# Expert weights split only in a branch where the expert changes, and 1.15 instead of 3.2 channel units beside each expert block

## The chip, the cores and the metric

The kernel runs on one core of a Trainium2 chip. The metric is the device time of one execution in microseconds. The profiled execution is one execution with its own time; the median of three others is given beside it.

## What is computed

Three stages follow each other on 4608 tokens of width 512. An attention with pooled keys gives the rows `x`. A mixture of eight experts then gives each token one expert: a fresh arg-max of its logits, or that of the token before it where the local gate says so. Last comes a layer norm with a channel feed-forward network on every token, with a residual.

```python
for b in range(B):
    prev_e = -1
    for s in range(S):
        fresh_e = int(np.argmax(logits[b, s]))
        if s == 0 or local_gate[b, s] < 0.5:
            e = fresh_e
        else:
            e = prev_e if prev_e >= 0 else fresh_e
        prev_e = e
        h = np.maximum(x[b, s] @ w1[e], 0.0)
        out[b, s] = p[e] * (h @ w2[e])
...
ch = np.maximum(xn @ w_ch1, 0.0) @ w_ch2
return (x + ch).astype(np.float32)
```

`w1[e]` is 512 x 1024 and `w2[e]` 1024 x 512, `w_ch1` 512 x 2048 and `w_ch2` 2048 x 512. For the drawn inputs the eight experts hold 1662, 912, 833, 596, 355, 221, 29 and 0 tokens when they are put in order of their size; this follows from the reference's own arithmetic. In blocks of 128 tokens these are 13, 8, 7, 5, 3, 2, 1 and 0 blocks, 39 in all.

## The kernel before, in words

Every product is made of three float16 products: each float32 operand is **split** into a high half (a scaled copy, on ScalarE) and a low half (the difference, on VectorE, or GpSimd in some places), and high x high, high x low and low x high are summed in PSUM. For expert weights this is `split_pair` (lines 532 to 548): ScalarE at line 534, VectorE at line 539, or GpSimd at lines 542 and 543, on pieces of 128 x 1024. `f1` and `f2` hold one expert's float32 weights as they come from HBM, `s1` and `s2` their two halves. There is one buffer of each, so that a new split has to wait until the matmuls that read the old one are done, and a new load until the split that reads `f1` or `f2` is done.

After the attention (to about 158 us of the profile) the **routing** part counts the tokens of each expert, sorts the experts by size and makes index tables (lines 647 to 850). Its end on VectorE is a row of small operations: `gidx`, `bsel` (which expert has block k), `ek`, `echg` (1 where the expert of block k is another than that of block k-1), `eoff` (its number), and then the low halves of the first expert's weights (`lows[2:4]`, line 780). At line 833 a block count is read into registers, and at line 834 stands a branch for more than 39 blocks, which every engine has to come to. Behind it `xprep_pe` transposes blocks 0 and 1 on TensorE (line 565), and the ScalarE and VectorE parts of the `f2` split are issued. The remaining halves of that split, `lows2[1::2]` at lines 1124 to 1126, are done by GpSimd (lines 542 and 543) within the first block.

The **main loop** (lines 1113 to 1171) goes over 39 expert blocks. The order is written out by hand, and each engine and each DMA queue keeps to the order of the program. In block k TensorE has: 12 matmuls of the first product for the first half of the hidden width (`moe1(k, 0)`, line 610), 12 of the second product of the block before (`moe2(k-1, 0)`, line 623), then `moe1(k, 1)`, then `moe2(k-1, 1)`. `moe1_out` (lines 613 to 618) follows each `moe1`: ScalarE makes the high half of the relu (line 614), VectorE the low half (line 615), and SyncE issues a DMA that transposes it into `hT` (line 616), which the `moe2` one block later reads. The PSUM tiles of `moe1` come from a pool of two, `ps_m`; from block 7 on the output of `moe2` takes its tile from the same pool (line 886), so that `moe1(k, 1)` needs the tile that `moe1(k, 0)` had.

From block FIRST = 8 on, **channel units** are put in between: `unit()` (lines 1025 to 1036) gives TensorE 12 matmuls of the first product of the feed-forward network (`ffn1`, line 939) and 12 of the second (`ffn2`, line 958) for the unit two before. There are 144 units. `mix(k, n)` (line 1103) gives one unit if fewer than `int(RATE * (k - FIRST) + n)` were given; it is called with n = 1 ahead of `moe1(k, 1)`, with n = 2 and 3 after `moe2(k-1, 1)`, and with n = RATE. What is left of the 144 units runs after the loop (lines 1172 to 1179). **Conversions** of the 32 pieces of the network's weights, which come as 64-bit floats, are made by `conv_a` (three VectorE operations, lines 119 to 126) and `conv_b` (two on ScalarE, one on GpSimd at line 132); `conv_slot` and `convert` place them: two for each block below block 8, and four from there on. Pieces 13 on share one buffer, `ct2`, so that the `conv_a` of one waits for the GpSimd part of the one before. `ln` (lines 899 to 929) is the layer norm of 128 tokens, taken from `yload`, whose transfer is issued by SyncE behind the scatter of `y_d`.

The expert weights, before: the first expert's are loaded once its number is known (lines 694 to 699). Below block SAME = 5 nothing is split, since the largest expert has at least five blocks. For blocks 4 to 12 `splits_if(k)` (lines 1062 to 1082) has one branch for each block, on whether the largest expert has ended; in it all pieces are split, a part of them on GpSimd. From block LIM = 13 on `splits1` and `splits2` split all eight pieces for every block, without a branch. Loads are issued for every block from 5 on by SyncE with a condition (`cond`), and move nothing where the expert stays.

Of the kernel before, what the change touches and what calls it, by code (L numbers as in the profile page):

```python
# [11 lines left out]
I32 = mybir.dt.int32  # L12
U32 = mybir.dt.uint32
AF = mybir.ActivationFunctionType
ALU = mybir.AluOpType
AX = mybir.AxisListType
# [3 lines left out]
B, H, S, D = 8, 8, 576, 64  # L20
# [3 lines left out]
NE, DF = 8, 1024  # L24
# [11 lines left out]
for _n, _w in (  # L36
    ("ident", 128), ("iota_nb", NB), ("kp128", NB), ("iota_e", NE), ("iota_e8", NE), ("first", NT), ("pcol", 1),
    ("maskv", 12), ("tri", 128), ("iota", 128),
):
    CST[_n] = (NCST, _w)  # L40
    NCST += _w
NKEEP = CST["maskv"][0]
SAME = (T // NE + 127) // 128
FRESH = -1.5 * 2.0 ** -23
# [3 lines left out]
def tile_attention_moe_ffn(ctx: ExitStack, tc: tile.TileContext, a, out):  # L48
# [7 lines left out]
    eoff = const.tile([1, NB], I32, name="eoff")  # L56
    echg = const.tile([1, NB], I32, name="echg")
    nbf = const.tile([1, 1], I32, name="nbf")
# [14 lines left out]
    def early(*shape, dt=F32):  # L73
# [8 lines left out]
    ident, iota_nb, kp128, iota_e, iota_e8, first, pcol = (  # L82
        cst[:, CST[n][0]:CST[n][0] + CST[n][1]] for n in ("ident", "iota_nb", "kp128", "iota_e", "iota_e8", "first", "pcol")
# [424 lines left out]
    def load_e(k):  # L508
        e = nc.sync.value_load(eoff[0:1, k:k + 1], min_val=0, max_val=NE - 1)
        c = nc.sync.value_load(echg[0:1, k:k + 1], min_val=0, max_val=1)  # L510
        ereg[k] = (e, c)
# [13 lines left out]
    def tick(n=1):  # L525
        while chains and n:
            if next(chains[0], None) is None:
                chains.pop(0)
            else:
                n -= 1  # L530

    def split_pair(f, s, c, o, pool, n=0):
        hi, lo, src = s[:, 0, c:c + 2, o:o + 512], s[:, 1, c:c + 2, o:o + 512], f[:, c:c + 2, o:o + 512]
        A.activation(out=hi, in_=src, func=AF.Copy, scale=SW)  # L534

        def low(pool):
            v = 2 - pool
            if v:
                V.scalar_tensor_tensor(out=lo[:, 0:v], in0=src[:, 0:v], scalar=SW, in1=hi[:, 0:v], op0=ALU.mult, op1=ALU.subtract)  # L539
            for x in range(v, 2):  # L540
                t = wp.tile([128, DM], F32, tag="xn", name="ptmp")
                nc.gpsimd.tensor_scalar(out=t, in0=src[:, x], scalar1=SW, scalar2=1.0, op0=ALU.mult, op1=ALU.mult)
                nc.gpsimd.tensor_tensor(out=lo[:, x], in0=t, in1=hi[:, x], op=ALU.subtract)

        if pool is None:
            return low
        low(int(pool))
        tick(n)
# [91 lines left out]
    with ExitStack() as rt:  # L640
# [108 lines left out]
        V.tensor_reduce(out=nbf, in_=nbl[0:1], axis=AX.X, op=ALU.max)  # L749
# [29 lines left out]
        V.tensor_copy(out=eoff, in_=ek[0:1])  # L779
        for f in lows[2:4]:  # L780
            f(0)
# [62 lines left out]
        for c in range(8, 8, 2):  # L844
            load_f2(0, c)
# [13 lines left out]

    LAG = 2  # L860
    LASTU = 7
    hf2 = [None]
    RATE = 3.2
# [5 lines left out]
    LIM = FIRST + 5  # L869
# [149 lines left out]
    def convert(k, n=0):  # L1019
        return k >= FIRST or (ncv[0] < EARLY and n % 2 == 0)  # L1020
# [16 lines left out]

    def splits1(k, half):
        if k >= NF:
            return  # L1040
        if half == 0 and SAME <= k + 1 < NF:
            load_e(k + 1)
        for c in (0, 2):
            if k >= LIM:
                split_pair(f1, s1, c, 512 * half, False, 2)
            else:
                tick(2)
            if SAME <= k + 1 < NF and not SAME <= k < LIM:
                load_f1(k + 1, c, 512 * half)

    def splits2(k, c0, c1):
        if k >= NF:
            return
        for c in range(c0, c1, 2):
            if k >= LIM:
                split_pair(f2, s2, c, 0, False, 2)
            elif k:
                tick(2)
            if SAME <= k + 1 < NF and not SAME <= k < LIM:
                load_f2(k + 1, c)  # L1060

    def splits_if(k):
        w1, w2 = SAME <= k + 1 < LIM, SAME <= k < LIM
        if not (w1 or w2):
            return
        if "nbf" not in ereg:
            ereg["nbf"] = nc.values_load(nbf[0:1, 0:1], min_val=0, max_val=NB)
        with tc.If(ereg["nbf"] < k + 2):
            if w1:
                for o in (0, 512):  # L1070
                    for c in (0, 2):
                        split_pair(f1, s1, c, o, c == 2)
            if w2:
                for c in range(0, 8, 2):
                    split_pair(f2, s2, c, 0, c % 4 == 2)
        if w1:
            for o in (0, 512):
                for c in (0, 2):
                    load_f1(k + 2, c, o)
        if w2:  # L1080
            for c in range(0, 8, 2):
                load_f2(k + 1, c)
# [30 lines left out]
    for k in range(NF + 1):  # L1113
# [10 lines left out]
        if k == 0:  # L1124
            for f in lows2[1::2]:
                f(2)
        norm_next(k)
# [13 lines left out]
        if k >= 1:  # L1141
            moe2(k - 1, 1)
            splits_if(k)
            splits2(k, 0, 4)
            yout(k - 1)
# [40 lines left out]
def host_layout(q, k, v, moe_w_gate, moe_w_local, moe_w1, moe_w2, moe2_g_ln, moe2_w_ch1, moe2_w_ch2):  # L1186
# [15 lines left out]
    for j in range(4):  # L1202
# [9 lines left out]
        "first": (128 * np.arange(NT)[None, :] + p[:, None]) % S == 0, "pcol": p[:, None],  # L1212
# [23 lines left out]
```

## Time and profile before

| | us |
| --- | --- |
| runs | 1365.77, 1366.81, 1359.57 |
| median | 1365.77 |
| profiled execution, its own time | 1364.15 |
| its span, first to last instruction | 1362.0 |
| TensorE busy in the span | 1314.8 |
| VectorE, ScalarE, GpSimd busy | 740.5, 595.0, 351.7 |

The span is 2.15 us shorter than the time of the same execution. Matmuls are pipelined, and their ends are modelled; so the number of matmuls in a stretch tells more than its busy time. PE is TensorE, PEld its weight loads, DVE VectorE, ACT ScalarE, POOL GpSimd, SP SyncE; a name with a q behind it is the engine's queue, where branches, register loads and semaphore instructions run.

### The profile page before, as it was taken

The numbers are of one execution on the slowest core, as the hardware profiler recorded it, in microseconds if no ns is written. First come the engines' busy times: TensorE is split into PE (matmuls) and PEld (weight loads), VectorE is DVE, ScalarE is ACT, GpSimd is POOL, SyncE is SP. The second block draws the span as 40 slices with busy tenths as digits, with TensorE's granted clock in tenths as the row PEclk, the third lists the DMA queues.
The fourth block names the chain that finished last, engine by engine and source line by source line (L and its number), as shares of the span: only waits on it lengthen the run. The fifth ranks groups of instructions, "written<-read, shape, count | busy, mean of one in ns | idle before, by whom it ended". The sixth has DMA issues, their size and how long they took to land. (4 is left out here: it accounts for less than half of the span.)

```text
span 1362.0 us, 19190 instructions
## 1 busy us (share of the span) xinstructions
PE 1314.8 (97%) x6512; PEld 663.0 (49%) x6512; DVE 740.5 (54%) x1540; ACT 595.0 (44%) x1107; POOL 351.7 (26%) x378
## 2 busy tenths in 40 slices
PE   5999889899999999999999999999999999999997
PEld 5999544444444444444444444444444444444443
DVE  6777885655575565656556655665566432131211
ACT  5788444534454454455435544554455422122110
POOL 3666263533341221122111211121121011020101
PEclk9999889999999999999999999999999999999999
DMA  8997358878573333256222453244356421020000
GB/s 269 306 295 250 109 174 169 174 164 178 144 227 78 78 78 71 71 132 135 68 71 73 113 125 105 70 121 118 100 147 172 106 70 47 8 70 24 32 0 32
DMA packets 211082, 162.49 MB, mean 119 GB/s; under 512 B 163422, under 2 KB 171870, under 8 KB 210976
## 3 DMA queue, kind: packets, MB, share of 16 engines
q1 hardware_dynamic: 197248, 115.10, 33.7%
q0 software_dynamic: 9120, 29.30, 7.2%
q10 hardware_dynamic: 4608, 16.78, 4.6%
q8 instruction: 53, 0.87, 0.3%
q14 instruction: 53, 0.43, 0.1%
HBM read 212.08 MB, written 29.28 MB: 177 GB/s over the span
## 5 line engine op out<-in xcount | busy, mean ns | idle before, releaser
L939 PE MATMUL f_ps<-xnT,c_sb 128*128 128x512 f16 x1728 | 395.8, 379 | 0.2 <-DVE hf L949 0.2
L958 PE MATMUL a<-c_sb,hf 128*128 128x512 f16 x1680 | 385.6, 379 | 0.0
L949 DVE SCALAR_TENSOR_TENSOR hf<-f_ps,hf 128x512 f16<-128x512 f32 x140 | 96.6, 690 | 343.6 <-ACT hf L948 343.6
L539 DVE SCALAR_TENSOR_TENSOR s<-f,s 128x1024 f16<-128x1024 f32 (+1 forms) x217 | 260.8, 1235 | 25.5 <-ACT s L534 25.5
L939 PEld LDWEIGHTS <-c_sb 128*128 128x128 f16 x1728 | 169.1, 98 | 204.2 <-issue 0.4
L958 PEld LDWEIGHTS <-hf 128*128 128x128 f16 x1680 | 164.4, 98 | 198.2
L948 ACT ACTIVATE hf<-f_ps 128x512 f16<-128x512 f32 x140 | 83.5, 597 | 403.3 <-PE f_ps L939 403.3
L610 PE MATMUL h_ps<-s,xT 128*128 128x512 f16 x936 | 216.6, 381 | 6.2 <-DVE hs L615 2.8
L623 PE MATMUL y_ps<-s,hT 128*128 128x512 f16 x936 | 216.4, 381 | 4.9 <-DMA hT<-hs 4.9
L534 ACT ACTIVATE s<-f 128x1024 f16<-128x1024 f32 x220 | 219.1, 1047 | 0.2 <-DMA f<-in_w_dram 0.2
L623 PEld LDWEIGHTS <-hT 128*128 128x128 f16 x936 | 91.5, 98 | 118.1 <-DMA hT<-hs 7.8
L610 PEld LDWEIGHTS <-xT 128*128 128x128 f16 x936 | 92.0, 98 | 117.2 <-issue 8.4
L614 ACT ACTIVATE hs<-h_ps 128x512 f16<-128x512 f32 x78 | 46.4, 595 | 163.3 <-PE h_ps L610 148.1
L615 DVE SCALAR_TENSOR_TENSOR hs<-h_ps,hs 128x512 f16<-128x512 f32 x78 | 53.8, 690 | 111.5 <-ACT hs L614 108.0
L922 POOL TENSOR_TENSOR xns<-xn,xns 128x512 f16<-128x512 f32 x36 | 41.7, 1158 | 256.3 <-ACT xns L921 243.6
L966 POOL DMA_INDIRECT out_dram<-yt,ti x36 | 41.0, 1139 | 186.7 <-DVE yt L965 148.7
L631 POOL DMA_INDIRECT y_d<-yr,sidx x39 | 40.8, 1045 | 166.8 <-ACT yr L629 138.8
L911 POOL TENSOR_TENSOR rs<-rs,mhalf 128x1 f32<-128x1 f32 x36 | 20.9, 581 | 216.0 <-DVE rs L910 216.0
L302 ACT ACTIVATE p<-s,nm 128x72 f32<-128x72 f32 x288 | 65.6, 337 | 7.6 <-DVE nm L288 7.5
L278 PE MATMUL s<-kb,qt 128*128 128x144 f32 (+1 forms) x320 | 47.2, 307 | 17.2 <-ACT kb L202 17.1
L557 POOL DMA_INDIRECT xg<-xrow_d,gidx x39 | 57.8, 1483 | 16.4 <-issue 8.7
L336 PE MATMUL o<-v,pt 128*128 128x148 f32 (+1 forms) x320 | 51.9, 298 | 3.5 <-DVE r L355 3.1
(187 smaller groups left out, 1018.9 us busy)
## 6 DMA issues: line engine op xcount, KB each, us to landing
f<-in_w_dram SPq DMA_DIRECT2D x280, 512.0 KB
xrow_d<-xr SPq DMA_DIRECT2D x36, 260.5 KB
yt<-y_d SPq DMA_DIRECT2D x36, 256.5 KB
kt<-in_kT_dram SPq DMA_DIRECT2D x16, 576.0 KB
qt<-in_qT_dram SPq DMA_DIRECT2D x18, 512.0 KB
vt<-in_vP_dram SPq DMA_DIRECT2D x16, 512.0 KB
c_sb<-in_c_dram ACTq DMA_DIRECT2D x16, 512.0 KB
shared<-in_c_dram ACTq DMA_DIRECT2D x8, 512.0 KB
```

Of the source, the lines that this page charges most:

```text
L302: nc.scalar.activation(out=p32[:, h, :], in_=s[:, h // 4, NK * (h % 4):NK * (h % 4) + NK], func=AF.Exp, bias=nm[:, h:h + 1],)
L336: nc.tensor.matmul(out=o[c][lo:hi, 2 * VC * e:2 * VC * (e + 1)], lhsT=pt[:, 2 * c + e, lo:hi], rhs=vb[:, 4 * c + 2 * e:4 * c + 2 * e + 2, ...
L534: A.activation(out=hi, in_=src, func=AF.Copy, scale=SW)
L539: V.scalar_tensor_tensor(out=lo[:, 0:v], in0=src[:, 0:v], scalar=SW, in1=hi[:, 0:v], op0=ALU.mult, op1=ALU.subtract)
L557: nc.gpsimd.indirect_dma_start(out=xg_t[k], out_offset=None, in_=xrow_d[:, :], in_offset=bass.IndirectOffsetOnAxis(ap=gidx[:, k:k + 1], ax ...
L610: nc.tensor.matmul(out=ps, lhsT=xT[:, x, c], rhs=s1[:, w, c, 512 * half:512 * half + 512], start=(n == 0), stop=(n == 11))
L615: V.scalar_tensor_tensor(out=hs[:, 1], in0=ps, scalar=0.0, in1=hs[:, 0], op0=ALU.max, op1=ALU.subtract)
L623: nc.tensor.matmul(out=ps, lhsT=hT[:, f // 4, x, f % 4], rhs=s2[:, w, f], start=(f == 0 and x + w == 0), stop=(f == 7 and x == 1),)
L939: nc.tensor.matmul(out=ps, lhsT=c1_sb[:, w, c, 128 * f:128 * f + 128], rhs=xT[:, x, c], start=(n == 0), stop=(n == 11))
L948: A.activation(out=hf[:, 0], in_=ps, func=AF.Relu)
L949: V.scalar_tensor_tensor(out=hf[:, 1], in0=ps, scalar=0.0, in1=hf[:, 0], op0=ALU.max, op1=ALU.subtract)
L958: nc.tensor.matmul(out=acc_t[t], lhsT=hf_t[u][:, x, 128 * t:128 * t + 128], rhs=c2_sb[:, w, f], start=(f == 0 and n == 0), stop=(f == NC2 ...
```

## The change

The branch of `splits_if`, `LIM` and the count `nbf` go. Instead, three words `chgw` are made in the routing part: bit k of them tells that the expert changes at block k. Every engine reads them into registers (`chg_r`). `splits1` and `splits2` have a branch of their own for each block from 5 on: four for each block, with two pieces in each, none of them on GpSimd. A table `enxt` gives the number of the next expert in order. The loads bring the weights of the next expert as soon as those of the present one are split, also at the start: the second expert's `f1` ahead of the loop, and its `f2` within block 0, after `lows2[1::2]`. `RATE` falls from 3.2 to 1.15, and `convert` gives two conversions for a block, not four, from block 8 on.

```diff
+WB = 15
+NW = (NB + WB - 1) // WB
...
-    nbf = const.tile([1, 1], I32, name="nbf")
+    ints = const.tile([1, 3 * NB + NW], I32, name="ints")
+    eoff, enxt, echg, chgw = (ints[:, NB * x:min(NB * x + NB, 3 * NB + NW)] for x in range(4))
...
     def load_e(k):
-        e = nc.sync.value_load(eoff[0:1, k:k + 1], min_val=0, max_val=NE - 1)
+        e = nc.sync.value_load(enxt[0:1, k:k + 1], min_val=0, max_val=NE - 1)
...
-        V.tensor_reduce(out=nbf, in_=nbl[0:1], axis=AX.X, op=ALU.max)
...
         V.tensor_copy(out=eoff, in_=ek[0:1])
+        chf = sb("chf", NW * WB)
+        V.memset(chf[0:1], 0.0)
+        V.tensor_tensor(out=chf[0:1, 0:NB], in0=echg, in1=pow2[0:1], op=ALU.mult)
+        chs = sb("chs", NW)
+        V.tensor_reduce(out=chs[0:1], in_=chf[0:1].rearrange("p (w b) -> p w b", b=WB), axis=AX.X, op=ALU.add)
+        V.tensor_copy(out=chgw, in_=chs[0:1])
+        rank = sb("rank", NE)
+        V.tensor_reduce(out=rank, in_=prec, axis=AX.X, op=ALU.add)
+        V.tensor_scalar(out=shf, in0=rank, scalar1=1.0, scalar2=None, op0=ALU.add)
+        nxm = sb("nxm", NE, NE)
+        V.tensor_tensor(
+            out=nxm, in0=rank.unsqueeze(1).to_broadcast([128, NE, NE]), in1=shf.unsqueeze(2).to_broadcast([128, NE, NE]), op=ALU.is_equal,
+        )
+        V.tensor_tensor(out=nxm, in0=nxm, in1=iota_e.unsqueeze(1).to_broadcast([128, NE, NE]), op=ALU.mult)
+        V.tensor_reduce(out=rank, in_=nxm, axis=AX.X, op=ALU.add)
+        V.tensor_tensor(out=ge, in0=bsel, in1=eb(rank), op=ALU.mult)
+        V.tensor_reduce(out=ek, in_=ge, axis=AX.X, op=ALU.add)
+        V.tensor_copy(out=enxt, in_=ek[0:1])
         for f in lows[2:4]:
             f(0)
...
     V.memset(mhalf, -0.5)
 
+    ereg[0] = nc.sync.value_load(enxt[0:1, 0:1], min_val=0, max_val=NE - 1), None
+    for o in (0, 512):
+        for c in (0, 2):
+            load_f1(0, c, o)
+    chg_r = [nc.values_load(chgw[0:1, w:w + 1], min_val=0, max_val=2 ** WB - 1) for w in range(NW)]
...
-    RATE = 3.2
+    RATE = 1.15
...
-    LIM = FIRST + 5
...
     def convert(k, n=0):
-        return k >= FIRST or (ncv[0] < EARLY and n % 2 == 0)
+        return n % 2 == 0 and (k >= FIRST or ncv[0] < EARLY)
...
+    def changes(k):
+        return tc.If((chg_r[k // WB] & (1 << (k % WB))) != 0)
+
     def splits1(k, half):
         if k >= NF:
             return
-        if half == 0 and SAME <= k + 1 < NF:
-            load_e(k + 1)
-        for c in (0, 2):
-            if k >= LIM:
-                split_pair(f1, s1, c, 512 * half, False, 2)
-            else:
-                tick(2)
-            if SAME <= k + 1 < NF and not SAME <= k < LIM:
-                load_f1(k + 1, c, 512 * half)
+        if k >= SAME:
+            if half == 0:
+                load_e(k)
+            with changes(k):
+                for c in (0, 2):
+                    split_pair(f1, s1, c, 512 * half, False)
+            for c in (0, 2):
+                load_f1(k, c, 512 * half)
+        tick(4)
 
     def splits2(k, c0, c1):
         if k >= NF:
             return
-        for c in range(c0, c1, 2):
-            if k >= LIM:
-                split_pair(f2, s2, c, 0, False, 2)
-            elif k:
-                tick(2)
-            if SAME <= k + 1 < NF and not SAME <= k < LIM:
-                load_f2(k + 1, c)
-
-    def splits_if(k):
...
+        if k >= SAME:
+            with changes(k):
+                for c in range(c0, c1, 2):
+                    split_pair(f2, s2, c, 0, False)
+            for c in range(c0, c1, 2):
+                load_f2(k, c)
+        if k:
+            tick(4)
...
         if k == 0:
             for f in lows2[1::2]:
                 f(2)
+            for c in range(0, 8, 2):
+                load_f2(0, c)
...
             moe2(k - 1, 1)
-            splits_if(k)
             splits2(k, 0, 4)
             yout(k - 1)
```

## Rows read from the trace of the kernel before

**Rows 1.** Busy time of the engines, share of the span, instructions (page).
```profile
PE 1314.8 (97%) x6512; PEld 663.0 (49%) x6512; DVE 740.5 (54%) x1540; ACT 595.0 (44%) x1107; POOL 351.7 (26%) x378
```

**Rows 2.** Stretches: length, busy time (count) by engine, granted clock, DMA share, GB/s.
```profile
185.00:350.00 165.00, 153.77 (x702) 69.51 (x703) 102.00 (x241) 74.12 (x128) 73.27 (x76) 0.98 0.76 161
350.00:1360.00 1010.00, 1004.82 (x4656) 455.35 (x4654) 496.41 (x828) 400.76 (x562) 185.00 (x192) 1.00 0.36 90
...
220.00:224.00 4.00, 4.00 (x13) 1.46 (x11) 2.01 (x8) 2.00 (x4) 2.13 (x2) 0.61 1.01 221
...
1350.00:1400.00 50.00, 4.82 (x23) 1.97 (x21) 1.39 (x2) 0.00 (x0) 1.93 (x2) 0.93 0.03 11
```

**Rows 3.** TensorE's waits, 185 to 350 us: us in total, times, longest.
```profile
PE y_ps L623 <- DMA hT<-hs: 4.9, 6, 2.2
PE h_ps L610 <- DVE hs L615: 2.8, 2, 2.5
PE h_ps L610 <- DVEq L1068: 2.3, 2, 1.8
...
PE h_ps L610 <- ACTq L1068: 1.1, 1, 1.1
```

**Rows 4.** TensorE in order of time: start, length, operation, [idle before, releaser].
```profile
211.66 2.76 PE L623 MATMUL y_ps<-s,hT 128*128 128x512 f16 x12 [0.64 <-DMA hT<-hs]
...
219.63 4.16 PE L623 MATMUL y_ps<-s,hT 128*128 128x512 f16 x12 [2.18 <-DMA hT<-hs]
223.58 3.09 PE L610 MATMUL h_ps<-s,xT 128*128 128x512 f16 x12
...
254.33 1.89 PE L610 MATMUL h_ps<-s,xT 128*128 128x512 f16 x8 [1.80 <-DVEq L1068]
257.25 2.76 PE L623 MATMUL y_ps<-s,hT 128*128 128x512 f16 x12 [1.03 <-DMA hT<-hs]
...
311.80 4.13 PE L610 MATMUL h_ps<-s,xT 128*128 128x512 f16 x12 [2.53 <-DVE hs L615]
```

**Rows 5.** The end of the routing on VectorE, and TensorE's wait for it.
```profile
181.77 0.51 DVE L776 TENSOR_REDUCE ek<-c_sb 128x43 f32<-128x344 f32 x1
182.31 0.19 DVE L778 TENSOR_TENSOR echg<-ek 1x42 int32<-1x42 f32 x1
...
184.99 0.64 PE L565 MATMUL tps<-shared,xg 128*128 128x128 f32 x4 [1.57 <-DVEq L834]
```

**Rows 6.** Register loads on the engines' queues: durations in ns, start.
```profile
L1067 PEldq TENSOR_LOAD <-nbf x1: 316/316/316, 236.0 to 236.0; - x1
...
L833 DVEq TENSOR_LOAD <-nbt x1: 545/545/545, 182.5 to 182.5; - x1
```

**Rows 7.** Block 0 on GpSimd and VectorE; the first weights' transfer, 164 to 180 us.
```profile
198.91 1.16 POOL L543 TENSOR_TENSOR s<-ptmp,s 128x512 f16<-128x512 f32 x1
...
195.95 0.68 DVE L615 SCALAR_TENSOR_TENSOR hs<-h_ps,hs 128x512 f16<-128x512 f32 x1
...
DMA packets 2180, 4.24 MB, mean 265 GB/s; under 512 B 128, under 2 KB 128, under 8 KB 2176
```

**Rows 8.** The branch of `splits_if`: min/median/max in ns, first and last start.
```profile
L1068 PEldq COMPARE_BRANCH  x10: 70/202/327, 236.5 to 392.6; - x10
...
L1068 DVEq EVENT_SEMAPHORE  x8: 21/21/21, 240.9 to 369.4; - x8
```

**Rows 9.** VectorE in block 9, in order of time.
```profile
309.26 0.43 DVE L122 TENSOR_SCALAR ct<-shared 128x512 uint32<-128x512 uint32 x1 [2.58 <-POOL c_sb L132]
...
311.06 0.68 DVE L615 SCALAR_TENSOR_TENSOR hs<-h_ps,hs 128x512 f16<-128x512 f32 x1
```

**Rows 10.** Splits and relu by line, 412 to 1080 us: busy, mean ns, idle before.
```profile
L539 DVE SCALAR_TENSOR_TENSOR s<-f,s 128x1024 f16<-128x1024 f32 x198 | 235.2, 1221 | 22.6 <-ACT s L534 22.6
...
L534 ACT ACTIVATE s<-f 128x1024 f16<-128x1024 f32 x198 | 197.4, 1048 | 0.0
...
L614 ACT ACTIVATE hs<-h_ps 128x512 f16<-128x512 f32 x50 | 29.9, 597 | 135.8 <-PE h_ps L610 122.4 <-issue 13.4
```

More of the change, by code (lines that the diff above doesn't have):

```diff
@@ L37 @@
     ("ident", 128), ("iota_nb", NB), ("kp128", NB), ("iota_e", NE), ("iota_e8", NE), ("first", NT), ("pcol", 1),
-    ("maskv", 12), ("tri", 128), ("iota", 128),
+    ("pow2", NB), ("maskv", 12), ("tri", 128), ("iota", 128),
 ):
@@ L55, in tile_attention_moe_ffn @@
     bsel = const.tile([128, NB, NE], F32, name="bsel")
-    eoff = const.tile([1, NB], I32, name="eoff")
-    echg = const.tile([1, NB], I32, name="echg")
-    nbf = const.tile([1, 1], I32, name="nbf")
+    ints = const.tile([1, 3 * NB + NW], I32, name="ints")
+    eoff, enxt, echg, chgw = (ints[:, NB * x:min(NB * x + NB, 3 * NB + NW)] for x in range(4))
     c1_sb = const.tile([128, 2, 4, DC], F16, name="c1_sb")
@@ L81, in tile_attention_moe_ffn @@
     cst = early(NKEEP)
-    ident, iota_nb, kp128, iota_e, iota_e8, first, pcol = (
-        cst[:, CST[n][0]:CST[n][0] + CST[n][1]] for n in ("ident", "iota_nb", "kp128", "iota_e", "iota_e8", "first", "pcol")
+    ident, iota_nb, kp128, iota_e, iota_e8, first, pcol, pow2 = (
+        cst[:, CST[n][0]:CST[n][0] + CST[n][1]] for n in ("ident", "iota_nb", "kp128", "iota_e", "iota_e8", "first", "pcol", "pow2")
     )
@@ L530, in tick, with split_pair @@
                 n -= 1
-    def split_pair(f, s, c, o, pool, n=0):
+    def split_pair(f, s, c, o, pool):
         hi, lo, src = s[:, 0, c:c + 2, o:o + 512], s[:, 1, c:c + 2, o:o + 512], f[:, c:c + 2, o:o + 512]
@@ L547, in split_pair @@
         low(int(pool))
-        tick(n)
     xg_t, lg_t, xT_t, pr_t, ex_t, hs_t, hT_t = {}, {}, {}, {}, {}, {}, {}
@@ L843, in tile_attention_moe_ffn @@
                     split_pair(f1, s1, c, o, False)
-        for c in range(8, 8, 2):
-            load_f2(0, c)
         for k in range(2):
@@ L1053, in splits2 @@
             return
-        for c in range(c0, c1, 2):
-            if k >= LIM:
-                split_pair(f2, s2, c, 0, False, 2)
-            elif k:
-                tick(2)
-            if SAME <= k + 1 < NF and not SAME <= k < LIM:
-                load_f2(k + 1, c)
-    def splits_if(k):
[L1063 to L1082, printed above, removed]
+        if k >= SAME:
[6 more added lines that the diff above has]
+            tick(4)
     pexp(0)
@@ L1211, in host_layout @@
         "iota_e": np.tile(np.arange(NE), (128, 1)), "iota_e8": np.tile(np.arange(NE) - NE, (128, 1)),
-        "first": (128 * np.arange(NT)[None, :] + p[:, None]) % S == 0, "pcol": p[:, None],
+        "pow2": np.tile(2.0 ** (np.arange(NB) % WB), (128, 1)), "first": (128 * np.arange(NT)[None, :] + p[:, None]) % S == 0, "pcol": p[:, None],
     }
```

## The prediction

> **What bounds the kernel now.** I read the busy times first: TensorE is busy for 1314.8 of 1362 us, and no other engine for more than 54% [rows 1]. That is an average over stages, so the table of stretches comes next. From 350 us on TensorE has 4656 matmuls in 1004.82 busy us, 215.8 ns each, with the clock granted in full (2.4 GHz); the 5.2 us that the stretch is short of 1010 lie behind the last matmul, since 4.82 us of work are left after 1350 us [rows 2]. So behind 350 us TensorE is never idle, and the change gives it neither fewer nor other matmuls. Whatever VectorE, ScalarE or SyncE save there is worth nothing by itself. From 185 to 350 us TensorE is idle for 165 − 153.77 = 11.2 us [rows 2]. The waits name them: 4.9 for transposed hidden halves, 2.8 for the low half of the relu, 2.3 + 1.1 for engines that had yet to come to the old branch [rows 3]. After two of these waits the next matmuls run slow: 12 take 4.16 us instead of 2.76, the next 12 3.09, after 2.18 us of idleness; the granted clock there is 0.61, so part of the stretch is at 1.2 GHz [rows 2, 4]. That is 1.4 + 0.35 = 1.75 us, and as much again after 2.53 us of idleness at 311.8 us. All that can be won between 185 and 350 us is 11.2 + 3.5 = 14.7 us, 1.1% of the time.
>
> The sum stands against the profiled execution's own 1364.15 us, 1.6 us below the median shown and inside the runs' spread.
>
> **Splits and rate.** 26 blocks are split before without need, 8 x (1.22 + 1.05) us each on VectorE and ScalarE [rows 10]. They are taken away behind TensorE's full stretch: nothing gained. Of 39 blocks the expert changes at 13, 21, 28, 33, 36 and 38; the branch of before agrees (8 bumps of a passed branch in blocks 4 to 11, and the body entered at 12, when 13 blocks of the largest expert are nearly over) [rows 8]. RATE only moves units: 12 matmuls take 2.59 us (12 x 215.8 ns), a block 10.4, a unit 5.2. A block with its units falls from 10.4 + 3.2 x 5.2 = 27 to 16.3 us; units not given in the loop (about 107, not 45) run behind it at the same pace. Cost nothing, as long as 16.3 us cover a block's other work.
>
> **The start, added to VectorE.** Twelve small operations stand ahead of `lows[2:4]`. Two are like `ek` (0.51), six are small (0.06 to 0.19, say 0.9 together), four work on 64 elements, which I put between these, 0.22 each: 1.02 + 0.9 + 0.88 = 2.8 us [rows 5]. TensorE waits just there for VectorE to reach the block-count branch [rows 5], so all of it is on the path. The count `nbf` that goes stood where VectorE waits anyway.
>
> **Three register loads** on each engine, behind the transposes of block 1 and ahead of block 0: 3 x 0.32 us; a load on VectorE took 0.55 [rows 6]. Bounds 0 (TensorE's queue runs ahead) and 1.6; here it has just been released and has no work queued, so I take 1.0.
>
> **The second expert's `f2` loads in block 0.** SyncE issues in order, and these four loads stand ahead of the transposing DMA of block 0's second half. The last of them must wait until GpSimd has read `f2`: 198.91 + 1.16 = 200.07 us, while that half is ready at 195.95 + 0.68 = 196.63 [rows 7]. Both ends move alike, so the DMA is issued 3.4 us later, and behind 0.5 MB, which at the first load's 265 GB/s takes 2.0 us [rows 7]. TensorE did not wait for it before, so up to about 2 us of the delay is slack. Between 1.4 and 5.4 us; I take 4.0, with the 1.75 us of slow clock as after the other long waits [rows 4]: 5.7. By a sentence of the Trainium skill (DMA: Bandwidth & Descriptors, queues, rings and completion order) each DMA engine takes the descriptors of a ring in their order, which would make the 2.0 us a real wait; no row here shows it.
>
> **Waits that this absorbs.** The 2.18 us wait at 219.63 and a smaller one of 0.6 ahead of it come from VectorE and ScalarE being behind TensorE in blocks 1 to 3. When TensorE stands still for 4 us more, they catch up: −(0.6 + 2.2 + 1.75) = −4.5 [rows 4], or nothing.
>
> **The old branch.** Its 3.4 us of waits [rows 3] go, since the new branches stand half a block ahead of the matmuls that need them. But the 1.80 us wait is followed within one product by 1.03 for a transposing DMA [rows 4]: that DMA would be waited for instead. I keep 1.6 (0 to 3.4).
>
> **Half the conversions.** At 309.26 VectorE stands 2.58 us on GpSimd for the single buffer of the conversions, its relu half comes behind that at 311.06 [rows 9], and TensorE loses 2.53 + 1.75 us [rows 4]. With two conversions in a block the buffer is free in time. −3.3 (up to −4.3; a unit less stands ahead of `moe1(9, 1)`, so I keep 1 back).
>
> **Blocks 9 to 17**, where conversions go on: mostly there is no unit left between `moe1(k, 0)` and `moe1(k, 1)`, whose PSUM tile is the one just used. The relu halves, 0.60 [rows 10] and 0.68 us [rows 7], then have one product for themselves, 2.59 us: 1.3 to spare. The conversion ahead of them on VectorE takes 1.8 us [rows 9]. It starts behind the relu of the block's unit, so 2.59 − 1.28 = 1.3 us before the block ends, and is over 0.5 us into the next, before the relu is due. I take 1.5 us in all, between 0 and nine times the 2.53 of block 9, 23 us. At block 13 two pieces per quarter of a block come on top, 2.4 us on VectorE against quarters of 4 us [rows 10]: 2 us (0 to 5). Later changes meet no conversions: 0.
>
> **The branches.** 136 (four in each of blocks 5 to 38), not 9. On TensorE's queue one takes 0.2 us (median, the last at 392.6) [rows 8], yet there is no idle time after 350 us [rows 2], so queued matmuls hide it: 0. The Trainium skill (Runtime: NRT & Kernel Launch, instruction fetch mechanics) says that a taken branch whose target lies outside the fetched window stops for a fetch. By that, some of the 136 would cost far more than 0.2 us; none of the ten here took over 0.33 us there [rows 8].
>
> **Sum:** 2.8 + 1.0 + 5.7 − 4.5 − 1.6 − 3.3 + 1.5 + 2.0 = +3.6: 1367.8, say 1368 us.
>
> **Rivals.**
> *Faster (0.13).* The `f2` loads don't hold anything up (the first half-block's slack takes it) and every early wait but that of the second transposing DMA goes: +3.8 for the routing and register loads, −12.2 (4.3 + 3.4 + 4.5): 1356. For it: these waits are all of the kind that the change moves. Against it: a removed wait that stands right ahead of another.
> *The relu halves become the bound (0.20).* In the conversion blocks the low half comes too late for the next product in each of the nine blocks, at 2.53 us: 1364 + 2.1 + 23 = 1389. It decides as soon as line 615 ends more than 2.6 us behind the last matmul of `moe1(k, 0)`. For it: block 9 of before shows just this wait, even with a unit in between [rows 4, 9]. Against it: that came from four conversions on one buffer.
> *A dearer start (0.12).* Nothing is absorbed and the `f2` wait costs its full 7.2 us: 1364 + 3.8 + 7.2 + 1.5 + 2 − 3.3 = 1375.
> *Branches on TensorE's path (0.05).* 136 x 0.2 = 27 us: 1395; it needs the queue to run empty in every quarter. A fetch by the rule named above would come to the same side.
> *The change does not do what it says (0.02).* If the bodies were entered in every block, VectorE would have 8 x 1.22 = 9.8 us of splits in each 16.3; a microsecond lost in each of 31 blocks gives 1399.
> The forecast keeps 0.48.
>
> **The range.** The lower ends of all terms give 1356, the upper ends past 1400. 1357 to 1384 leaves out the far part of the relu rival, the branches and a little of the fast case. A measurement of this kernel can tell about 0.5%, 6.8 us, from no change: faster means below 1359, slower above 1372.6. Faster 0.13; slower 0.20 + 0.12 + 0.05 + 0.02 − 0.02 (relu waits that stay small) = 0.37; same 0.50.
>
> **What would show it.** Matmuls at 216 ns without idleness from about block 10 to the end; the transposes of block 1, at 184.99 before [rows 5], about 3 us later and the first expert matmul another one; a wait for `hT` of some 4 us at the end of block 1; no wait on a branch; no slow stretch near 311 us; the loop over about 31 x 10.7 = 330 us earlier. Wrong it would be by a repeated wait on line 615 or 614 ahead of line 610 in blocks 9 to 17, by TensorE standing on VectorE at blocks 13, 21 or 28, or by gaps at branches.

## The result, and the profile after

The changed kernel takes 1374.38 us (median of 6 runs, 1369.81 to 1379.85), the kernel before 1359.94 us beside it (6 runs, 1357.82 to 1366.81). The ratio is 1.0101, with a 95% interval of 1.0078 to 1.0123: slower by 1.0%, 14.4 us. That is inside the range of 1357 to 1384 us, but of the three outcomes it is the one that was given 0.37, not the likeliest. The profiled execution took 1379.85 us, the slowest of the six, so lengths of its stages are read against other profiles below.

The busy line of the page for the kernel after, against [rows 1]:

```profile
PE 1319.3 (96%) x6512; PEld 662.7 (48%) x6512; DVE 555.0 (40%) x1387; ACT 447.7 (32%) x943; POOL 329.0 (24%) x374
```

VectorE has 185.5 us less to do, ScalarE 147.3 us less, and the kernel is slower. TensorE has the same 6512 matmuls. What counts is where it stands still. Its waits from 178 us on (total, times, longest), against [rows 3]:

```profile
PE y_ps L623 <- DMA hT<-hs: 11.8, 4, 6.9
PE h_ps L610 <- DVE hs L615: 6.9, 4, 2.4
PE tps L565 <- DVEq L851: 4.0, 1, 4.0
PE y_ps L623 <- ACT s L535: 1.9, 1, 1.9
PE h_ps L610 <- ACTq L1067: 1.6, 1, 1.6
PE y_ps L623 <- DVE s L540: 1.1, 2, 0.9
```

The two waits on line 540 and the one on line 535 are new in kind: TensorE waits for a split of expert weights. In order of time, TensorE after (start, length, operation, idle before and releaser), against [rows 4] and the last of [rows 5]:

```profile
184.50 1.12 PE L565 MATMUL tps<-shared,xg 128*128 128x128 f32 x4 [3.96 <-DVEq L851]
185.65 7.41 PE L610 MATMUL h_ps<-s,xT 128*128 128x512 f16 x24
197.51 2.76 PE L623 MATMUL y_ps<-s,hT 128*128 128x512 f16 x12 [1.43 <-DMA hT<-hs]
...
203.82 2.76 PE L623 MATMUL y_ps<-s,hT 128*128 128x512 f16 x12 [0.96 <-DMA hT<-hs]
...
222.88 4.24 PE L623 MATMUL y_ps<-s,hT 128*128 128x512 f16 x12 [2.47 <-DMA hT<-hs]
...
264.08 4.87 PE L623 MATMUL y_ps<-s,hT 128*128 128x512 f16 x12 [6.95 <-DMA hT<-hs]
...
296.44 2.75 PE L610 MATMUL h_ps<-s,xT 128*128 128x512 f16 x12 [2.38 <-DVE hs L615]
...
378.50 2.75 PE L610 MATMUL h_ps<-s,xT 128*128 128x512 f16 x12 [1.61 <-DVE hs L615]
396.02 2.75 PE L610 MATMUL h_ps<-s,xT 128*128 128x512 f16 x12 [1.81 <-DVE hs L615]
791.01 2.75 PE L610 MATMUL h_ps<-s,xT 128*128 128x512 f16 x12 [1.06 <-DVE hs L615]
801.91 2.53 PE L623 MATMUL y_ps<-s,hT 128*128 128x512 f16 x11 [0.17 <-DVE s L540]
806.30 0.38 PE L623 MATMUL y_ps<-s,hT 128*128 128x512 f16 x1 [1.86 <-ACT s L535]
807.57 4.22 PE L623 MATMUL y_ps<-s,hT 128*128 128x512 f16 x11 [0.88 <-DVE s L540]
```

The first 24 expert matmuls of the kernel before:

```profile
185.47 5.34 PE L610 MATMUL h_ps<-s,xT 128*128 128x512 f16 x24
```

Three places are to be seen. At the start the wait ahead of the transposes has grown from 1.57 to 3.96 us, and the 24 matmuls behind it take 7.41 us where they took 5.34. In blocks 1 to 8 there are still long waits. And behind 350 us, where TensorE of before was never idle [rows 2], there are six waits of 7.4 us in all. The table of stretches has the same (length, then busy time and count by engine, granted clock, DMA share, GB/s), first before, then after:

```profile
350.00:450.00 100.00, 100.00 (x465) 45.35 (x464) 62.53 (x101) 44.46 (x67) 31.68 (x30) 1.00 0.55 150
...
800.00:1000.00 200.00, 200.00 (x928) 90.66 (x927) 118.27 (x192) 96.26 (x132) 42.02 (x43) 1.00 0.42 110
```

```profile
350.00:450.00 100.00, 96.57 (x448) 43.57 (x447) 54.40 (x106) 41.85 (x70) 30.36 (x32) 1.00 0.81 177
...
800.00:1000.00 200.00, 197.09 (x905) 88.78 (x903) 46.72 (x101) 37.38 (x58) 28.41 (x31) 0.99 0.18 49
```

Before, the two stretches hold 465 and 928 matmuls; after, 17 and 23 of them are missing, and each takes 0.216 us.

What stood ahead of the late waits, on VectorE of the kernel after in order of time:

```profile
780.06 0.69 DVE L927 BATCH_NORM_STATS2 bs<-yt 128x6 f32<-128x512 f32 x1 [6.97 <-DMA yt<-y_d]
...
799.03 0.69 DVE L927 BATCH_NORM_STATS2 bs<-yt 128x6 f32<-128x512 f32 x1 [8.07 <-DMA yt<-y_d]
```

VectorE stands 7 and 8 us on the row that layer norm loads. Behind it in its queue are the splits and relu halves that TensorE needs when the expert changes at blocks 36 and 38.

In block 8 it is ScalarE that stands, ahead of the relu half that TensorE waits for at 296.44:

```profile
295.07 0.60 ACT L614 ACTIVATE hs<-h_ps 128x512 f16<-128x512 f32 x1 [5.11 <-DMA f<-in_w_dram]
```

The profile names a load of expert weights as what released it, in a block at which the expert does not change. Why ScalarE had to wait for it was not followed up.

**Stages, by landmarks in TensorE's order of time.** Three landmarks are the transposes at the end of the attention (line 654), the first expert matmul, and the first `ffn1` matmul, in block 8. From the first to the second before took 27.35 us and after 31.12 us; from there to the first unit 97.05 and 105.66; from there to the last matmul 1072.30 and 1079.91. Of the middle stage one profile says little: seven profiles whose code is alike up to block 8, but for the number of branches in one (the changed kernel and six of the runs below), lie between 98.9 and 106.8 us, mean 102.8; two of the old code there are 97.05 and 94.7. The other two stages repeat: five profiles of the changed start take between 31.11 and 31.13 us, the other two 31.40 and 31.43, and the run below that has only more branches takes 1079.85 us in the last stage.

### The profile page after: what moved, and what is told of

It is laid out like the page before. It is cut to its first block, busy times and chain, and to the rows that moved or that the text cites. A ratio compares the mean times of both kernels' runs of the same rounds, so it can differ in the third digit from the quotient of the medians.

```text
span 1377.9 us, 20409 instructions
## 1 busy us (share of the span) xinstructions
PE 1319.3 (96%) x6512; PEld 662.7 (48%) x6512; DVE 555.0 (40%) x1387; ACT 447.7 (32%) x943; POOL 329.0 (24%) x374
## 5 line engine op out<-in xcount | busy, mean ns | idle before, releaser
L623 PE MATMUL y_ps<-s,hT 128*128 128x512 f16 x936 | 220.4, 386 | 14.7 <-DMA hT<-hs 11.8
L986 POOL DMA_INDIRECT out_dram<-yt,ti x36 | 35.4, 984 | 355.9 <-DVE yt L985 312.5
L540 DVE SCALAR_TENSOR_TENSOR s<-f,s 128x1024 f16<-128x1024 f32 x53 | 63.8, 1242 | 19.4 <-ACT s L535 18.5
L535 ACT ACTIVATE s<-f 128x1024 f16<-128x1024 f32 x56 | 55.7, 1047 | 0.0
L940 ACT ACTIVATE xn<-yt,rs 128x512 f32<-128x512 f32 x36 | 29.3, 814 | 79.3 <-DVE rs L934 72.7
```

Source lines behind the costliest of these rows:

```text
L623: nc.tensor.matmul(out=ps, lhsT=hT[:, f // 4, x, f % 4], rhs=s2[:, w, f], start=(f == 0 and x + w == 0), stop=(f == 7 and x == 1),)
```

## The experiments

The theory after the result: the low rate, with the blocks that it makes short, costs what was lost behind block 8; the table operations and the early loads cost what was lost ahead of it; the branches cost nothing. The rivals: the branches themselves (136 on each engine), the halved conversions, or the start alone. The kernel before was measured again beside each group of runs, with medians between 1358.99 and 1363.74 us, so runs of different groups are compared by their ratios; a difference of their times in us is rougher.

**RATE 3.2 and the old conversions, all else as changed.**

```diff
-    RATE = 1.15
+    RATE = 3.2
-        return n % 2 == 0 and (k >= FIRST or ncv[0] < EARLY)
+        return k >= FIRST or (ncv[0] < EARLY and n % 2 == 0)
```

> The changed kernel with 3.2 units and four conversions for a block again; branches, tables and the second expert's early loads stay. Theory of the cover: the waits of the changed kernel at blocks 12 to 14 (1.6 + 1.8 us) and 36 to 38 (4.0 us and 1.5 of slow clock) are there because a block is too short to hide splits, conversions and layer norms, so they go: 9 us less than the changed kernel's 1374, 1365, ratio to before near 1.004. Rival, branches or tables hold the whole loss: the time stays at 1372 to 1375.

Measured: 1366.72 us (12 runs), ratio 1.0021 (1.0002 to 1.0040). All waits of TensorE behind 300 us are gone, and the last stage takes 1071.38 us, like before. The two kernels differ in nothing ahead of block 8, so the difference comes from rate and conversions: 0.8% or 10.9 us by the ratios, 1374.4 − 1366.7 = 7.7 us by the medians, and 1079.91 − 1071.38 = 8.5 us by the last stage of one profile each. That is the larger part of the 14.4 us. What is left, 0.2% here, is the start and blocks 0 to 8. VectorE's and ScalarE's saved time is in this kernel too (555.7 and 448.1 us busy), and is worth nothing. RATE 3.2 with half the conversions was not run, so the two edits are told apart at RATE 1.15 alone (below).

**Table operations and early loads behind the first blocks.** The 12 operations go behind `lows2[0::2]`, the register loads and the second expert's eight loads to block 3.

```diff
         for f in lows2[0::2]:
             f(0)
+        chf = sb("chf", NW * WB)
...
     for k in range(NF + 1):
+        if k == 3:
+            chg_r.extend(nc.values_load(chgw[0:1, w:w + 1], min_val=0, max_val=2 ** WB - 1) for w in range(NW))
+            ereg[0] = nc.sync.value_load(enxt[0:1, 0:1], min_val=0, max_val=NE - 1), None
+            for o in (0, 512):
+                for c in (0, 2):
+                    load_f1(0, c, o)
+            for c in range(0, 8, 2):
+                load_f2(0, c)
```

> The changed kernel with the twelve small VectorE operations behind the first halves of f2 instead of ahead of the low halves of f1, and the register loads and the second expert's loads at block 3. Theory of the start: the first expert matmul comes some 3.7 us earlier behind the routing, and the slow clock of the first 24 matmuls (2.1 us) goes: 1368 to 1370, ratio near 1.006. Rival, the start's loss is given back by waits in blocks 1 to 3 that are set by VectorE anyway: 1373 to 1375.

Measured: 1399.65 us (6 runs), ratio 1.0272 (1.0234 to 1.0311). A miss: the start's waits went as expected, and two dearer ones came. TensorE in order of time:

```profile
197.70 1.08 PE L565 MATMUL x_ps<-shared,xg 128*128 128x128 f32 x4 [8.73 <-DMA xg<-xrow_d,gidx]
...
252.59 5.00 PE L623 MATMUL y_ps<-s,hT 128*128 128x512 f16 x12 [15.50 <-DMA hT<-hs]
```

The first is a fault of the edit: GpSimd issued that gather only after 12.6 us of waiting for VectorE, probably because the later operations kept memory in use that the next gathers are written to; the trace shows the wait and not its reason. The second is a price: 4 MB of loads issued in one place stand on SyncE's queue ahead of a transposing DMA, and TensorE waits 15.5 us for that. Both are avoided in the next run of this kind.

**Layer norm two blocks behind its load, everywhere.**

```diff
-        if ready and (k >= FIRST or k >= ready[0][1] + 2):
+        if ready and (k >= NB or k >= ready[0][1] + 2):
```

> The changed kernel with the layer norm of 128 tokens started two blocks, not one, behind its load. Theory of the norm: VectorE stands 7 to 8 us on the load at blocks 36 and 38, and the splits behind it come too late; with a block more the waits at 791 to 808 us go: 4 to 5.5 us less, 1369 to 1370. Rival, those waits come from the splits of blocks 36 and 38 by themselves: 1373 to 1375, with the same waits.

Measured: 1376.06 us, ratio 1.0091 (1.0062 to 1.0121). The waits of 791 to 808 us are gone, but one came at the change of expert at block 13, where the transposing DMA of `xT` is late. On SyncE's queue weight loads that move data and a transposing DMA of layer norm stand ahead of it; which of them delays it was not tested. So the run decides nothing by its time. TensorE:

```profile
385.73 5.21 PE L610 MATMUL h_ps<-s,xT 128*128 128x512 f16 x12 [3.89 <-DMA xT<-xs]
```

**The same from block 20 on only**, so that block 13 is left as it was.

```diff
-        if ready and (k >= FIRST or k >= ready[0][1] + 2):
+        if ready and (k >= NB or FIRST <= k < 20 or k >= ready[0][1] + 2):
```

> The changed kernel with layer norm two blocks behind its load from block 20 on only (blocks 9 to 19 as in the changed kernel, so that the change of expert at 385 us, where the same edit everywhere brought a wait of 3.9 us, is not touched). Theory (the two waits for layer norm's load at 780 and 799 us, behind which the splits of the last changes of expert queue, cost some 5 us of the low rate's loss): no wait of TensorE after 450 us, ratio 1.005 to 1.008. Rival (what they cost is won back in the time that the last stage takes, or another wait takes their place): ratio as the changed kernel's, 1.010, with a wait of TensorE between 700 and 850 us.

Measured: 1373.03 us (8 runs), ratio 1.0078 (1.0049 to 1.0106). No wait of TensorE is left behind 450 us, the last stage takes 1075.22 us against 1079.91, so 4.7 us for the late waits and their slow matmuls. (The four late waits and the slow matmuls behind the last sum to 5.7 us in the changed kernel's profile.) By the times it is less sure: the ratio is 0.23% lower, 3 us, with intervals that overlap. The rest of the last stage's loss is 1075.22 − 1072.30 = 2.9 us: the waits in blocks 8, 12 and 14 (5.8 us in this profile, and 1.7 of slow matmuls) less the 4.3 us of the kernel before in block 9 [rows 4].

**Each branch cut in two**, 272 in place of 136.

```diff
-            with changes(k):
-                for c in (0, 2):
+            for c in (0, 2):
+                with changes(k):
                     split_pair(f1, s1, c, 512 * half, False)
```

> The changed kernel with each branch cut in two: eight for a block, 272, the same splits. Theory that branches cost nothing: 1373 to 1376. Rival, a branch costs on the path: if the 136 branches hold 9 us or more of the loss, 136 more cost as much again, 1383 or above.

Measured: 1379.88 us (6 runs), between the two forecasts, but the kernel before took 1363.74 us beside it: ratio 1.0109 (1.0075 to 1.0143), the changed kernel's 1.0101; the last stage 1079.85 us against 1079.91. Twice the branches cost nothing that can be measured. Their records in the changed kernel on one line of the two (min, median, max in ns, first and last start):

```profile
L1067 PEldq COMPARE_BRANCH  x80: 66/207/340, 234.2 to 776.1; - x80
L1067 ACTq COMPARE_BRANCH  x80: 34/45/45, 239.0 to 785.2; - x80
...
L1067 DVEq COMPARE_BRANCH  x80: 43/56/63, 240.1 to 788.0; - x80
```

No branch on TensorE's queue is longer than 0.34 us, and queued matmuls cover that.

**All conversions, with RATE 1.15 kept.**

```diff
-        return n % 2 == 0 and (k >= FIRST or ncv[0] < EARLY)
+        return k >= FIRST or (ncv[0] < EARLY and n % 2 == 0)
```

> The changed kernel with the old number of conversions (every slot, not half), RATE 1.15 kept: of the two edits that were undone together it undoes one. Theory (the low rate costs, not the conversions): the waits behind the layer norm's load at some 790 to 808 us stay (4 to 5 us and their slow clock), ratio 1.006 to 1.011. Rival (the half conversions cost, because they last longer, into the blocks in which an expert changes at 369 to 396 us): those waits go and the ratio falls to 1.003 or less.

Measured: 1398.51 us (6 runs), ratio 1.0262 (1.0221 to 1.0304). Both theories fall: the halved conversions don't cost, they save 1.6%. TensorE in blocks 9 to 13:

```profile
314.64 4.44 PE L610 MATMUL h_ps<-s,xT 128*128 128x512 f16 x12 [4.16 <-DVE hs L615]
336.76 5.28 PE L610 MATMUL h_ps<-s,xT 128*128 128x512 f16 x12 [4.73 <-DVE hs L615]
358.43 2.75 PE L610 MATMUL h_ps<-s,xT 128*128 128x512 f16 x12 [3.03 <-DVE hs L615]
380.65 4.24 PE L610 MATMUL h_ps<-s,xT 128*128 128x512 f16 x12 [6.52 <-DVE hs L615]
```

And VectorE ahead of the last of these:

```profile
373.67 0.43 DVE L123 TENSOR_SCALAR ct<-shared 128x512 uint32<-128x512 uint32 x1 [1.76 <-DMA shared<-in_c_dram]
...
378.12 0.43 DVE L123 TENSOR_SCALAR ct<-cw 128x512 uint32<-128x512 uint32 x1 [2.57 <-POOL c_sb L133]
378.58 0.69 DVE L125 SCALAR_TENSOR_TENSOR ct<-cw,ct 128x512 uint32<-128x512 uint32 x1
379.31 0.69 DVE L127 SCALAR_TENSOR_TENSOR ct<-cw,ct 128x512 uint32<-128x512 uint32 x1
379.92 0.68 DVE L615 SCALAR_TENSOR_TENSOR hs<-h_ps,hs 128x512 f16<-128x512 f32 x1
```

The relu half waits behind conversions, and these wait for their buffer and their data. This is the rival of the prediction in which the relu halves become the bound, in the kernel that lacks the third part of the change.

**RATE 2.0 with all conversions.**

```diff
-    RATE = 1.15
+    RATE = 2.0
```

and the conversions as in the run above.

> The changed kernel with RATE 2.0 and the old number of conversions, between two measured: 1.026 at RATE 1.15 and 1.002 at RATE 3.2, both with that number. Theory (a block of the loop holds one block's work of VectorE, and what TensorE has in a block shrinks with RATE; where VectorE's work is more, TensorE waits): the cost falls faster than in a straight line with RATE, since VectorE's 8 to 10 us conversions fit a block of some 19 us: ratio 1.002 to 1.008. Rival (each block in the loop costs the same whatever its length, in a straight line): 1.016.

Measured: 1378.27 us (6 runs), ratio 1.0104 (1.0065 to 1.0142). It lies between: under the straight line's 1.016, as the theory had it, and over the 1.008 that the theory allowed. The last stage says it without the first blocks: 1071.38, 1085.61 and 1100.58 us at RATE 3.2, 2.0 and 1.15, all with every conversion; the line would have 1088.5 at 2.0. So with every conversion the cost is somewhat under the straight line, and neither of the two lower rates is free.

**The kernel before with RATE 1.15 and half the conversions**, so without branch, tables and early loads; the two lines are those of the first run, the other way round.

> The kernel before with only RATE 1.15 and half the conversions: splits in every block as before, no branch of the new kind, no table operations. Theory (the branch is what makes a short block affordable): a block is about 16.4 us of TensorE and VectorE has some 10 us of splits in it, beside relu, layer norm and softmax work, so VectorE's queue runs late behind relu halves and TensorE waits in most blocks: ratio 1.015 to 1.04. Rival (VectorE keeps up, the low rate costs only where a layer norm load holds VectorE): ratio 1.005 to 1.010, as the changed kernel.

Measured: 1405.41 us (6 runs), ratio 1.0317 (1.0281 to 1.0353). TensorE's wait on the relu half in this kernel:

```profile
PE h_ps L610 <- DVE hs L615: 36.8, 15, 4.9
```

VectorE is late fifteen times. Eleven of these waits, 28.5 us, come from 375 us on, where splits run in every block. The other four, 8.3 us, come ahead of the first split of expert weights in the loop, which begins at 354.8 us on ScalarE, so splits are not their cause. The last of the four:

```profile
353.28 4.44 PE L610 MATMUL h_ps<-s,xT 128*128 128x512 f16 x12 [3.27 <-DVE hs L615]
```

Between 290 and 354 us VectorE stands 14.3 us on layer norm's load, in three waits; why that load is late here was not tested. The branch, with tables and early loads, takes the ratio from 1.0317 to 1.0101: the three together are worth some 29 us at this rate, and at RATE 3.2 the kernel that has them is 0.2% slower than the kernel before.

**The start's term: tables in block 1, loads spread over blocks 2 to 4.** The table tiles lie in memory that no gather uses; the loads go one or two at a time behind `moe1`.

```diff
+                chains.insert(1, tables())
...
         if k < NF:
             moe1(k, 0)
+            if 2 <= k < 5:
+                for _ in range(k // 4 + 1):
+                    second.pop(0)()
```

> The changed kernel with its 12 table operations moved behind the first blocks (they run on VectorE in block 1, from memory that no gather waits for), the register loads at block 3, and the second expert's eight 512 KB loads one or two at a time behind the transposing DMAs of blocks 2 to 4. RATE stays 1.15. Theory (start term is real: 3.1 us between the end of attention and the first matmul, and 2.1 us of the first 24 matmuls at the lower clock): about 5 us under the changed kernel, ratio to the kernel before about 1.006 instead of 1.010, the 24 matmuls take 5.34 us again and the wait ahead of them falls from 3.96 to under 2 us. Rival (the start is won back later, because TensorE has other waits in blocks 1 to 8): ratio stays within 0.002 of 1.010.

> The same moves, and RATE 3.2 with the old number of conversions beside them, so the changed kernel without its start and without its late waits. Theory (both terms are real and add): about 1361 us where the kernel before has 1364, ratio 0.996 to 1.000; after block 9 no wait of TensorE, before it waits of 10 us in all at most. Rival (the first nine blocks have a bound of their own that takes back what the start gives): ratio as with RATE 3.2 alone, 1.002.

Measured: with RATE 1.15 1380.35 us, ratio 1.0133 (1.0098 to 1.0168); with RATE 3.2 1367.89 us (12 runs), 1.0046 (1.0022 to 1.0071). The start did go back to 27.4 and 27.5 us, with its 24 matmuls at full clock, and nothing was won: the theory fails in both. The ratios lie above even those that the rivals named (1.010 within 0.002, and 1.002); the interval of the first reaches down to its rival, that of the second just does not. The two waits of TensorE with RATE 3.2 that took its place:

```profile
235.55 4.45 PE L623 MATMUL y_ps<-s,hT 128*128 128x512 f16 x12 [4.12 <-DMA hT<-hs]
257.11 5.30 PE L623 MATMUL y_ps<-s,hT 128*128 128x512 f16 x12 [3.72 <-DMA hT<-hs]
```

The middle stage takes 109.03 us in this profile, more than in any of the seven with the loads in block 0.

**The second expert's number early, its loads in block 0, tables in block 1.** Three VectorE operations find the second largest key, so that the loads need no table.

```diff
+        V.tensor_reduce(out=topf[0:1], in_=key[0:1], axis=AX.X, op=ALU.max)
+        V.scalar_tensor_tensor(out=key2[0:1], in0=key[0:1], scalar=topf[0:1, 0:1], in1=key[0:1], op0=ALU.is_lt, op1=ALU.mult)
+        V.tensor_reduce(out=sec, in_=key2[0:1], axis=AX.X, op=ALU.max)
```

> RATE 3.2 and the old number of conversions; the second expert's number comes from three small VectorE operations behind the first blocks' preparation, so its eight loads run in block 0 as in the changed kernel, where the transposing DMAs did not suffer from them; the 12 table operations run in block 1 and the registers are loaded at block 3. Theory (a start's gain was given back because the second expert's 4 MB went into blocks 2 to 4, in front of the transposing DMAs): with the loads in block 0 the gain stays: some 4 to 5 us under RATE 3.2 alone, ratio 0.997 to 1.001, first 24 matmuls in 5.34 us, waits on transposing DMAs no more than with RATE 3.2 alone (5.3 us). Rival (blocks 1 to 8 have a bound of their own, to which TensorE comes earlier and waits longer): ratio 1.002 to 1.005.

Measured: 1375.09 us (6 runs), ratio 1.0085 (1.0054 to 1.0115): a miss. The start is 27.46 us, the middle stage 115.68. TensorE's first wait in it:

```profile
199.24 5.11 PE L624 MATMUL y_ps<-s,hT 128*128 128x512 f16 x12 [8.20 <-DMA hT<-hs]
```

SyncE's issues tell why, first in this run and then in the changed kernel:

```profile
188.60 2.44 SPq L518 DMA_DIRECT2D f<-in_w_dram  x4
191.13 2.37 SPq L617 DMA_TRANSPOSE hT<-hs  x1
```

```profile
184.67 2.26 SPq L517 DMA_DIRECT2D f<-in_w_dram  x4
191.85 1.36 SPq L616 DMA_TRANSPOSE hT<-hs  x1
```

The first four loads, 2 MB, are issued 2.5 us ahead of the first transposing DMA here, and 7 us ahead of it in the changed kernel. At the 289 GB/s that all queues together moved between 190 and 200 us, 2 MB take about 7 us, an estimate; by it they have nearly landed there when the transposing DMA is issued. What the start gains in time it takes from these loads.

A rule of the Trainium skill (DMA: Bandwidth & Descriptors, queues, rings and completion order) says that each DMA engine takes the descriptors of one ring in their order. By it the transpose would stand behind the 2 MB, and the wait of 8.20 us agrees.

**The same with layer norm late.** The edit is that of the third run, on top of the last.

> The same, and layer norm two blocks behind its load. Theory (layer norm's scatter wait delays splits and with them the queues of blocks 5 to 8 alone): 2 to 3 us less than without it, ratio 0.995 to 0.999, because the long wait at an expert change that this edit brought at RATE 1.15 came from the short blocks there. Rival (it comes at the change of expert whatever the rate): 3 to 5 us more than without it.

Measured: 1418.97 us (6 runs), ratio 1.0421 (1.0389 to 1.0454): far outside both. At RATE 3.2 the units need the norm sooner, and TensorE waits for it instead:

```profile
PE f_ps L971 <- DMA xnT<-xns: 30.2, 4, 8.5
```

No version beat the kernel before. The nearest is the changed kernel with the old rate, at 1.0021.

## Why the prediction came out as it did

The range held, the mechanism of the first stage was right in kind, and the direction came out on the side that had 0.37. That the range held is in part luck: terms of the sum that did not come, in both directions, offset each other. By the steps:

- **TensorE full behind 350 us, so what other engines save is worth nothing.** Right, and shown by the run with RATE 3.2. The 26 blocks "split without need" are 20, since six of the 26 need their split: line 539 has 217 records before and its counterpart, line 540, 53 after, eight to a block. At a price of nothing it changes nothing in the sum.
- **Table operations, +2.8, and register loads, +1.0.** Right: from 178.99 to 182.05 us the twelve operations take 3.06, and the stage up to the first expert matmul grew by 31.12 − 27.35 = 3.77 us. What the step left out is the clock behind it: the granted clock was 0.65 between 178 and 190 us, and the 24 matmuls, in part at 1.2 GHz, took 2.07 us more. The prediction counted slow matmuls behind waits elsewhere and not here. The stretch with the clock (the 0.65):

```profile
178.00:190.00 12.00, 7.72 (x23) 3.11 (x22) 10.00 (x25) 4.94 (x7) 6.05 (x6) 0.65 0.45 142
```

- **`f2` loads ahead of a transposing DMA, +5.7.** Failed in size: the four `f2` loads stand ahead of the transposing DMA of block 0's second half, and TensorE waited 0.96 us for that, at 203.82, with no slow matmuls; before it did not wait there. The 1.43 us at 197.51 are for the first half, which has the `f1` loads ahead of it, a cost that the prediction left out (0.62 us before, without them). Against before, both loads cost 0.96 + 0.81 = 1.8 us. The prediction took the end of GpSimd's last subtraction [rows 7] for the moment at which `f2` is free. The instruction that reads `f2` is the scaling ahead of it. Its last record before, and after, on GpSimd:

```profile
197.86 0.96 POOL L542 TENSOR_SCALAR ptmp<-f 128x512 f32<-128x512 f32 x1
```

```profile
195.77 1.01 POOL L543 TENSOR_SCALAR ptmp<-f 128x512 f32<-128x512 f32 x1
```

  Besides, GpSimd's splits did not move with the rest: they end 2 us earlier though TensorE begins block 0 at the same time. So `f2` was free at 196.78 us, and the half that the DMA transposes was ready at about 196.9. The mechanism is real, though: where the `f1` loads came shortly ahead of the first half's transposing DMA, in the run that found the second expert early, TensorE waited 8.20 us.
- **Waits absorbed, −4.5, and the old branch, −1.6.** Not seen. There is a wait of 2.47 us at 222.88 in place of the 2.18 [rows 4], and in place of the old branch's waits one of 6.95 us at 264.08, which is 2.3 to 4.5 us in the six other profiles of that code. In the mean of the profiles the middle stage grew by 102.8 − 95.9 = 6.9 us, 2.1 of them the slow matmuls at its beginning, where the prediction summed −4.5 − 1.6 + 5.7 = −0.4. With the 3.8 us of the start that is 10.7 us ahead of block 8. By the times it is less: 14.4 − 7.7 = 6.7 us by the medians, 0.2% or 2.9 us by the ratio of the run with RATE 3.2. The exact share stays open, and so does the cause of the longer waits in blocks 1 to 8. The trace has one hint: SyncE's issue of the transposing DMA ahead of the 6.95 us took 4.78 us, where the median of its kind between 205 and 292 us is 1.24:

```profile
258.18 4.78 SPq L616 DMA_TRANSPOSE hT<-hs  x1
```

- **Half the conversions, −3.3.** Mis-sized, and put down to the wrong edit. The wait of 2.53 us in block 9 went, with its slow matmuls, and one of 2.38 us at full clock came at 296.44 in block 8: about 2.53 + 1.75 − 2.38 = 1.9 us won. But the run with RATE 3.2 and every conversion has the same (2.29 us in block 8, none in block 9), so halving did not bring it. What halving is worth shows only at the new rate, which the step did not ask: 1.0262 against 1.0101, 1.6%.
- **Blocks 9 to 17, +1.5, and block 13, +2.0.** Right in sum: 1.61 + 1.81 = 3.42 us at 378 and 396 us.
- **Later changes, 0.** The step that failed with the largest price behind block 8. "Later changes meet no conversions" was true, but conversions are not all that VectorE has: layer norm's load stood in front of the splits of blocks 36 and 38. Together with the slow matmuls it cost 4.7 us of the last stage, as the run with the norm late from block 20 on shows by its profile. A block of 16.3 us was taken to cover a block's other work by its busy time; a queue that stands 8 us on a DMA is not busy time.
- **Branches, 0.** Right; twice as many changed nothing. The rule of the Trainium skill (Runtime: NRT & Kernel Launch, instruction fetch mechanics), a fetch where a taken branch leaves the window, would have shown as branches far over the 0.34 us of the longest on TensorE's queue, or in the doubled count's time; neither is there.

Of the rivals, that in which the relu halves become the bound was the nearest in kind: it is what happens with all conversions, and what the third part of the change holds off. The sum of +3.6 came out at +14.4 us: two gains of 6.1 did not come, 2.1 of slow matmuls at the start and 4.7 at the last changes were left out, 1.4 of the conversions' gain was missing, and of the 5.7 for the loads 1.8 were paid. That makes +14.0, closer than these figures can bear: in the last stage the terms sum to 3.4 + 4.7 − 1.9 = 6.2 us of the 7.6 that it grew by, and between the start and block 8 they have 2.1 + 1.8 = 3.9 us of a mean of 6.9, where the profiles scatter over 8.

## What to carry to other kernels

Where TensorE is full, work taken from other engines is worth nothing, and an edit that spends that room, here shorter blocks, brought only waits: the low rate cost 3.2% in the kernel before, even with half the conversions, and the branch with its tables and early loads won most of it back, to 1.0%. Whether a short block covers its work is asked of each queue's longest stand, the loads it waits for included, not of its busy share. And a bulk load moved off one path lands ahead of something else on its queue: follow it to the next DMA that TensorE waits for.

## What the runs showed of the hardware that was not expected

- A wait of 3.96 us ahead of a handful of transposes was followed by 24 matmuls that took 7.41 us in place of 5.34, and one of 3.72 us by 12 in 5.30 in place of 2.75; the length of the wait alone does not tell, since one of 2.18 us was followed by 12 in 4.16 us [rows 4], one of 2.38 us by 12 in 2.75, and one of 3.03 us, in the run with all conversions, by 12 in 2.75.
- The first eight blocks of the same code differ by up to 6.7 us from one profiled execution to another (105.66 and 98.9 us, two kernels that are alike up to there), where the stage ahead of them repeats within 0.3 us.
- One branch takes 45 ns on ScalarE's queue, 56 on VectorE's and 207 on TensorE's (medians).
